# Attention in groups of two units, and no branch between two expert layers

## The chip, the cores and the metric

The kernel runs on one core of a Trainium2 chip. The metric is the device time of one execution in microseconds, as the median of several runs. The core has five engines that run beside each other, each through its own list of instructions in order: TensorE (matmuls; PE in the profile, with its weight loads as PEld), VectorE (DVE), ScalarE (ACT), GpSimd (POOL) and SyncE (SP), whose queue issues most of the DMAs. They wait for each other through semaphores.

## The reference

Three layers follow each other. The first is attention over 4 batches, 8 heads, 768 positions and 64 channels, with a window of 128 positions and 4 sink positions that every row sees:

```
keep = is_sink | in_window
scores = np.where(keep, scale * q @ k.T, -1e9)
a = softmax(scores)
x = (a @ v) as 3072 tokens of 512 channels
```

The second is a layer of 8 experts. Each token goes to the expert with the largest gate logit, and `out = gate * (relu(x @ w1[e]) @ w2[e])` with 1024 hidden channels. The third is such a layer again, but each expert takes exactly 384 tokens, in the order of all logits, largest first.

## The kernel before

**Attention** handles two heads (a pair) at a time: 16 pairs, and of each six blocks of 128 query rows. A block of a pair is a unit; there are 96. Two neighbouring units share an output tile and form a group; there are 48 groups. What is done for unit n is cut into steps, each a small function:

- `qk_mm` (line 291): scores of both heads on TensorE, 260 columns each (132 in the first unit of a pair), into one of two PSUM buffers `sp`;
- `mask_max` (lines 302 to 310): masks and row maximum on VectorE;
- `exp` (line 321): exponentials with row sums on ScalarE, which frees `sp`;
- `trans` (329): transposes of the exponentials into the PSUM tile `pt`; `sel` (335 to 340): copy of them to SBUF on ScalarE, and two selections on GpSimd that cut the window's lower and upper triangle into `lu`;
- `pv` (358): products of the values with `lu` into `po`;
- once a group: `sinkpack` (368), `sinktr` (375) and `sinkout` (380) for the sink columns, `outT` (386, copy of `po`), `rows` (396, 398, output rows and gate logits into the tile `px`), `xout` (412 to 418, division by the row sums on VectorE, store).

The order is written out by hand. A loop runs over units, and in each turn over a string of step names; each step has a lag in units, so that turn n does the scores of unit n, the exponentials of unit n-1, the transposes of unit n-2, the values products of unit n-6:

```
LM, LE, LT, LP, LK, LS, LO, LR = 0, 1, 2, 6, 3, 6, 8, 9
ORDER = "ex ld qk ini bg pv mm tr ro oT sp st xo so sq se"
```

So TensorE gets, for each unit, scores, values products, transposes, and then the group's output rows or the sink transpose. Two more steps are `ini`, which in the first turns prepares the sinks' values, and `bg`, which takes one piece of a background list (`BG`) in each of 108 turns. The list holds the setup of constants and, after each batch, the gate: logits, argmax, ranks, scatter of the token numbers; after the second batch also the table of the first experts' tiles, the gathers of their tokens, and one piece that loads their weights. What is left is taken in the first expert layer, two pieces at each tick while more than 12 are waiting.

**The first expert layer** (`moe1`) runs a static list of tiles. If an expert needs more tiles than the list has, further bodies run under a branch (line 1171) whose condition every engine loads from a table `tab`; with the inputs used here none of them runs. Then **the second expert layer** (`moe2`) selects the tokens by a search on VectorE with counts on TensorE (line 1375), loads the first expert's weights once its number is known, and runs the experts. At the end stands another branch, with a general version of the last layer that runs only if the search failed; it does not here.

Of the kernel before, what the change touches and what calls it, by code (L numbers as in the profile page):

```python
# [20 lines left out]
NB = S // 128  # L21
# [149 lines left out]
LM, LE, LT, LP, LK, LS, LO, LR = 0, 1, 2, 6, 3, 6, 8, 9  # L171
ORDER = "ex ld qk ini bg pv mm tr ro oT sp st xo so sq se"


def attention(ctx, tc, g, qT, kT, v4, vsT, vsR, wg, put_x, after_batch, bg, drain=True):
# [6 lines left out]
    NU = B * NP * NB  # L182
# [93 lines left out]
    st = {}  # L276

    def unit(n):
        p, i = divmod(n, NB)
        b, pr = divmod(p, NP)  # L280
        return b, pr, p, i

# [13 lines left out]
    def mask_max(n):  # L296
# [12 lines left out]
        s.mx = wk.tile([128, 2], F32, name="mx", bufs=3)  # L309
        nc.vector.tensor_reduce(s.mx, sp[:, :, 128:260], axis=AX.X, op=OP.max, negate=True)  # L310

    def exp(n):
        b, pr, p, i = unit(n)
        s = st[n]
        if i % 2 == 0:
            s.P = wk.tile([128, 2, 2, SEG], F32, name="P", bufs=4)
            s.sm = wk.tile([128, 2, 2], F32, name="sm", bufs=8)
        else:
            s.P, s.sm = st[n - 1].P, st[n - 1].sm
        for hd in range(2):  # L320
            nc.scalar.activation(s.P[:, i % 2, hd, :], s.sp[:, hd, 128:260], AF.Exp, bias=s.mx[:, hd:hd + 1],  # L321
                                 accum_out=s.sm[:, i % 2, hd:hd + 1])

    def trans(n):
        s = st[n]
        s.ptt = ps.tile([128, 512], F32, name="pt")
        s.pt = s.ptt[:, 0:256].rearrange("p (a c) -> p a c", a=2)
        for hd in range(2):
            nc.tensor.transpose(s.pt[:, hd, :], s.P[:, n % 2, hd, 4:132], g.ident)

    def sel(n):
        b, pr, p, i = unit(n)
        s = st[n]
        s.t = wk.tile([128, 2, 128], F32, name="t", bufs=3)
        nc.scalar.activation(s.t, s.pt, AF.Copy)
        s.lu = wk.tile([128, 2, 2, 128], F32, name="lu", bufs=8)
        nc.gpsimd.affine_select(s.lu[:, :, 0, :], s.t, pattern=[[0, 2], [1, 128]],
                                compare_op=OP.is_ge, fill=0.0, base=0, channel_multiplier=-1)
        if i:
            nc.gpsimd.affine_select(st[n - 1].lu[:, :, 1, :], s.t, pattern=[[0, 2], [-1, 128]],  # L340
                                    compare_op=OP.is_gt, fill=0.0, base=0, channel_multiplier=1)

    def pv(n):
        b, pr, p, i = unit(n)
        for j in ([i - 1] if i else []) + ([i] if i == NB - 1 else []):
            lu = st[n - i + j].lu
            if j == 0:
                st[p, 0] = ps.tile([128, 2, 128], F32, name="po", bufs=2)
            segs = [(0, 1)] if j == NB - 1 else ([(0, 2)] if j % 2 == 0 else [(0, 1), (1, 2)])
            for l0, l1 in segs:  # L350
                blk = j + l0
                gi = blk // 2
                if blk % 2 == 0 and l0 == 1:
                    st[p, gi] = ps.tile([128, 2, 128], F32, name="po", bufs=2)
                po = st[p, gi]
# [6 lines left out]
    def sinkpack(gn):  # L362
        s = st[2 * gn + 1]
        sk = psk[gn % 4]
        src = s.P[:, :, :, 0:4]
# [5 lines left out]
    def sinktr(gn, pt):  # L371
        s = st[2 * gn + 1]
        s.skp = (ps.tile([128, 512], F32, name="pt") if pt is None else pt)[0:96, 384:512]
        sk = psk[gn % 4]
        nc.tensor.transpose(s.skp, sk.bitcast(F32).rearrange("p a b c -> p (a b c)"), g.ident)

    def sinkout(gn):
        s = st[2 * gn + 1]
# [3 lines left out]
    def outT(gn):  # L382
        s = st[2 * gn + 1]
        p, gi = divmod(gn, 3)
        s.oT = wk.tile([128, 2, 128], F32, name="oT")
        nc.scalar.activation(s.oT, st[p, gi], AF.Copy)
# [3 lines left out]
    def rows(gn):  # L390
        s = st[2 * gn + 1]
        p, gi = divmod(gn, 3)
        b, pr = divmod(p, NP)
        s.px = ps.tile([128, 512], F32, name="px")
        px = s.px[:, 0:288].rearrange("p (a c) -> p a c", a=2)
        nc.tensor.matmul(px, s.skT, bd[:, p], start=True, stop=False, skip_group_check=True)
        for blk in range(2):
            nc.tensor.matmul(px[:, blk, :], s.oT[:, blk, :], rw[:, pr, :], start=False, stop=True,
                             skip_group_check=True)

    def xout(gn):
        s = st[2 * gn + 1]
        p, gi = divmod(gn, 3)
        b, pr = divmod(p, NP)
# [5 lines left out]
        px = s.px[:, 0:288].rearrange("p (a c) -> p a c", a=2)  # L410
# [5 lines left out]
                                px[:, :, 0:128].rearrange("p a (h d) -> p a h d", h=2),  # L416
                                bc(rv[:, :, :, None], [128, 2, 2, 64]), op=OP.mult)
        nc.vector.tensor_tensor(lp[:, i0:i0 + 2, h0:h0 + 2, :],
                                px[:, :, 128:144].rearrange("p a (h d) -> p a h d", h=2),
# [5 lines left out]

    def at(n, lag, last=NU):
        return n - lag if lag <= n < last + lag else None

    def sink(n, lag):
        m = n - lag  # L430
        return m // 2 if 0 <= m and m % 2 == 0 and m // 2 < NU // 2 else None

    def when(f, *a):
        return lambda n: None if f(n) is None else a[0](f(n))

    def loads(n):
        b, pr, p, i = unit(n)
        if i == 1:
            load_pair(p + 2)
            load_v(p + 1)  # L440

    def one_of(n, f):
        p, i = divmod(n, NB)
        f(p + 1, i)

    ops = dict(
        ld=when(lambda n: at(n, 0), loads),
        qk=when(lambda n: at(n, 0), qk_mm),
        mm=when(lambda n: at(n, LM), mask_max),
        ex=when(lambda n: at(n, LE), exp),  # L450
        tr=when(lambda n: at(n, LT), trans),
        se=when(lambda n: at(n, LT), sel),
        st=when(lambda n: sink(n, LS), lambda k: sinktr(k, st[2 * k + LS - LT].ptt if 2 * k + LS - LT < NU else None)),
        so=when(lambda n: sink(n, LS), sinkout),
        sp=when(lambda n: sink(n, LK), sinkpack),
        oT=when(lambda n: sink(n, LO), outT),
        ro=when(lambda n: sink(n, LR), rows),
        xo=when(lambda n: sink(n, LR), xout),
        pv=when(lambda n: at(n, LP), pv),
        sq=when(lambda n: at(n, 0), lambda n: one_of(n, scale_q)),  # L460
        bg=lambda n: bg.pop(1),
        ini=init)
    for n in range(NU + LR + 3):
        for op in ORDER.split():
            if op == "qk" and n < 6:
                warm(7 - n)
            ops[op](n)
# [10 lines left out]
class Gate:  # L478
    def __init__(self, tc, g, pool, mid, mbias, bg):
# [11 lines left out]
        self.tab = pool.tile([1, 3, NBIG + E], I32, name="tab")  # L491
# [601 lines left out]
def moe1(tc, g, G, src, rt, w1, w2, wg2, wg2T, x2d):  # L1093
    nc = tc.nc
    with ExitStack() as ctx:
# [4 lines left out]
        ids = src.ids  # L1100
        wgb = f.wk.tile([128, E, DM], F32, name="wgb", bufs=1)
        nc.sync.dma_start(wgb, bass.AP(tensor=wg2T.tensor, offset=wg2T.offset, ap=[[0, 128], [DM, E], [1, DM]]))
# [7 lines left out]
        def yout(j, a, y):  # L1110
            c = src.first(j)
            late = c - NMAIN if c is not None else -1
            yr = f.wk.tile([128, DM + E], F32, name=f"yr{(a + max(late, 0)) % 4}", bufs=1)
            lg = yr[:, DM:] if c is None else rt.LG[:, c + a]
            nc.scalar.activation(yr[:, 0:DM], y, AF.Copy, scale=src.gate(j, a))
            st = {}

            def dot(e):
                junk = f.wk.tile([128, DM], F32, name="junk")
                V.scalar_tensor_tensor(junk, yr[:, 0:DM], 1.0, wgb[:, e, :], op0=OP.mult, op1=OP.mult,  # L1120
                                       accum_out=lg[:, e:e + 1])
# [22 lines left out]
            def put():  # L1144
                nc.sync.dma_start(rt.xs[128 * (c + a):128 * (c + a) + 128, :], yr[:, 0:DM])

            def scatter():
                nc.gpsimd.indirect_dma_start(out=x2d, out_offset=bass.IndirectOffsetOnAxis(
                    ap=ids[j][:, a, 0:1], axis=0), in_=yr, in_offset=None, bounds_check=N - 1, oob_is_err=False)
            dots = [(lambda e=e: dot(e)) for e in range(E)]  # L1150
            if c is None:
                bg.add(*dots, scatter)
            elif j in static[:-3]:
                bg.add(put, *dots)
# [11 lines left out]
        def run(js, pre=None):  # L1166
            f.run(js, w1, w2, src, yout, hook=lambda: bg.pop(2 if len(bg.q) > 12 else 1), pre=pre, onx=onx, LEAD=2)

        run(static, (src.raw, dict(src.xg)))
# [742 lines left out]
```

## Time and profile before

| | |
|---|---|
| median of 3 runs | 937.57 us (936.87 to 937.63) |
| the profiled execution, its own time | 933.44 us |
| its span | 931.6 us |
| TensorE busy | 877.2 us, 94% |
| VectorE busy | 637.6 us, 68% |
| ScalarE busy | 419.8 us, 45% |
| GpSimd busy | 354.4 us, 38% |
| DMA, mean over the span | 133 GB/s |

The span is what the trace covers; the execution's own time lies 1.8 us above it. The shares are means over stages with different limits: attention ends at about 202 us, the first expert layer at about 539 us. In the trace a line such as L291 is a line of the kernel before, "x4" is the number of instructions in a row, `128*64` the part of the array that a matmul uses, and "<-PE sp L291" names what ended an engine's idle time. Matmuls are pipelined and their ends are modelled, so it is the starts that can be compared.

### The profile page before, as it was taken

The numbers are of one execution on the slowest core, as the hardware profiler recorded it, in microseconds if no ns is written. First come the engines' busy times: TensorE is split into PE (matmuls) and PEld (weight loads), VectorE is DVE, ScalarE is ACT, GpSimd is POOL, SyncE is SP. The second block draws the span as 40 slices with busy tenths as digits, with TensorE's granted clock in tenths as the row PEclk, the third lists the DMA queues.
The fourth block names the chain that finished last, engine by engine and source line by source line (L and its number), as shares of the span: only waits on it lengthen the run. The fifth ranks groups of instructions, "written<-read, shape, count | busy, mean of one in ns | idle before, by whom it ended". The sixth has DMA issues, their size and how long they took to land. (4 is left out here: it accounts for less than half of the span.)

```text
span 931.6 us, 15380 instructions
## 1 busy us (share of the span) xinstructions
PE 877.2 (94%) x5034; PEld 680.8 (73%) x5040; DVE 637.6 (68%) x1815; ACT 419.8 (45%) x1183; POOL 354.4 (38%) x600
## 2 busy tenths in 40 slices
PE   9999999988999999999998877999999998999993
PEld 4566666657888888888876635778888787789982
DVE  4878788757688878797954848878878777623220
ACT  4788887853333333343434504233424342344430
POOL 4676766753401010200000005536364563457441
PEclk9999999999999999999995979999999998999997
DMA  8244646394444444443443115326343442334201
GB/s 263 94 156 112 184 104 171 86 344 116 129 137 153 136 136 136 136 136 102 136 148 136 57 44 187 122 95 208 140 150 117 133 149 101 125 125 159 91 34 37
DMA packets 68951, 123.99 MB, mean 133 GB/s; under 512 B 9075, under 2 KB 21365, under 8 KB 68726
## 3 DMA queue, kind: packets, MB, share of 16 engines
q1 hardware_dynamic: 62166, 103.41, 34.8%
q0 software_dynamic: 6688, 19.43, 6.5%
q8 instruction: 44, 0.72, 0.3%
q14 instruction: 53, 0.43, 0.2%
HBM read 103.11 MB, written 19.71 MB: 132 GB/s over the span
## 5 line engine op out<-in xcount | busy, mean ns | idle before, releaser
L934 ACT ACTIVATE hh<-ph 128x384 fp32r<-128x384 f32 (+1 forms) x112 | 60.3, 538 | 270.9 <-PE ph L925 266.6
L925 PE MATMUL ph<-xh,w1h 128*128 128x384 f32 (+1 forms) x448 | 170.3, 380 | 0.0
L868 PE MATMUL y<-w2h,hh 128*128 128x512 f32 x400 | 163.8, 409 | 0.0
L925 PE MATMUL ph<-xh,w1l 128*128 128x384 f32 (+1 forms) x448 | 162.8, 364 | 0.0
L925 PE MATMUL ph<-xl,w1h 128*128 128x384 f32 (+1 forms) x448 | 161.9, 363 | 0.0
L868 PE MATMUL y<-w2h,hl 128*128 128x512 f32 x400 | 159.1, 398 | 0.0
L868 PE MATMUL y<-w2l,hh 128*128 128x512 f32 x400 | 159.0, 397 | 0.0
L935 DVE SCALAR_TENSOR_TENSOR hl<-ph,hh 128x384 fp32r<-128x384 f32 (+1 forms) x112 | 68.6, 612 | 109.6 <-ACT hh L934 106.7
L1080 POOL DMA_INDIRECT xg<-xd,ent x26 | 29.2, 1122 | 217.4 <-DMA ent<-idtab 118.9
L821 POOL TENSOR_TENSOR w2l<-w2r,w2h 128x512 fp32r<-128x512 f32 x64 | 87.5, 1372 | 53.3 <-ACT w2h L817 38.5
L1120 DVE SCALAR_TENSOR_TENSOR junk<-yr,wgb 128x512 f32<-128x512 f32 x160 | 103.6, 689 | 0.0
L925 PEld LDWEIGHTS ph<-xh,w1h 128*128 128x128 f32 x448 | 86.0, 192 | 10.7 <-issue 0.4
L925 PEld LDWEIGHTS ph<-xh,w1l 128*128 128x128 f32 x448 | 85.8, 192 | 9.6
L925 PEld LDWEIGHTS ph<-xl,w1h 128*128 128x128 f32 x448 | 85.2, 190 | 7.8
L868 PEld LDWEIGHTS y<-w2h,hl 128*128 128x128 f32 x400 | 76.3, 191 | 17.1 <-DVE hl L973 0.4
L868 PEld LDWEIGHTS y<-w2h,hh 128*128 128x128 f32 x400 | 76.7, 192 | 12.4 <-ACT hh L972 0.4
L868 PEld LDWEIGHTS y<-w2l,hh 128*128 128x128 f32 x400 | 76.6, 192 | 12.3 <-DVE w2l L821 0.3
L840 DVE TENSOR_TENSOR w1l<-w1r,w1h 128x512 fp32r<-128x512 f32 x96 | 73.6, 768 | 14.0 <-ACT w1h L835 13.0
L835 ACT ACTIVATE w1h<-w1r 128x512 fp32r<-128x512 f32 x128 | 79.7, 623 | 5.5 <-DMA w1r<-in_w_dram 2.8
L817 ACT ACTIVATE w2h<-w2r 128x512 fp32r<-128x512 f32 x128 | 79.4, 624 | 2.2 <-issue 2.2
L321 ACT ACTIVATE P<-sp,mx 128x132 f32<-128x132 f32 x192 | 69.0, 367 | 10.8 <-DVE mx L310 8.6
L840 POOL TENSOR_TENSOR w1l<-w1r,w1h 128x512 fp32r<-128x512 f32 x32 | 43.8, 1369 | 62.7 <-ACT w1h L835 62.7
(342 smaller groups left out, 1506.7 us busy)
## 6 DMA issues: line engine op xcount, KB each, us to landing
w1r<-in_w_dram SPq DMA_DIRECT2D x32, 1024.0 KB
w2r<-in_w_dram SPq DMA_DIRECT2D x32, 1024.0 KB
xs<-yr SPq DMA_DIRECT2D x26, 256.0 KB
kr<-in_kT_dram SPq DMA_DIRECT2D x16, 396.0 KB
qr<-in_qT_dram SPq DMA_DIRECT2D x16, 384.0 KB
vr<-in_v_dram SPq DMA_DIRECT2D x16, 384.0 KB
xd<-xb SPq DMA_DIRECT2D x16, 384.0 KB
wgb<-in_wg2T_dram SPq DMA_DIRECT2D x1, 2048.0 KB
```

The lines of the kernel that those rows point to most:

```text
L321: nc.scalar.activation(s.P[:, i % 2, hd, :], s.sp[:, hd, 128:260], AF.Exp, bias=s.mx[:, hd:hd + 1], accum_out=s.sm[:, i % 2, hd:hd + 1])
L817: nc.scalar.activation(ch[1][c][0], r[:, q, :], AF.Copy)
L821: eng.tensor_tensor(lo, r[:, q, :], h.bitcast(F32), op=OP.subtract)
L835: nc.scalar.activation(h, v, AF.Copy)
L840: eng.tensor_tensor(lo, v, h.bitcast(F32), op=OP.subtract)
L868: nc.tensor.matmul(o, l, r, start=(first and i == 0), stop=(end and i == 2))
L925: nc.tensor.matmul(ph, wp[:, c, :], xp_[:, c, 0:NTK], start=(d == 0 and i == 0), stop=(d == 3 and i == len(cut[d]) - 1))
L934: nc.scalar.activation(hh, ph, AF.Relu)
L935: nc.vector.scalar_tensor_tensor(hl, ph, 0.0, hh.bitcast(F32), op0=OP.max, op1=OP.subtract)
L1080: self.nc.gpsimd.indirect_dma_start(out=self.xg[j][:, a, :], out_offset=None, in_=self.G.xd[0:k, :], in_offset=bass.IndirectOffsetOnAxis(a ...
L1120: V.scalar_tensor_tensor(junk, yr[:, 0:DM], 1.0, wgb[:, e, :], op0=OP.mult, op1=OP.mult, accum_out=lg[:, e:e + 1])
```

## The change

The loop now runs over groups of two units. In each turn both units' scores are issued, then both masks and maxima, then the four transposes of the group before into one tile, with one copy of 512 elements between the two units' exponentials, the sink transpose and the output rows (which now share the tile `px`), and at the end both units' values products. The two selections of the lower triangle become one. The background list gives two pieces a turn, in 52 turns. The branch between the expert layers is gone: its bodies move into a function of their own, under the branch at the end.

```
-LM, LE, LT, LP, LK, LS, LO, LR = 0, 1, 2, 6, 3, 6, 8, 9
-ORDER = "ex ld qk ini bg pv mm tr ro oT sp st xo so sq se"
+LST, LPV, LRO = 3, 2, 4
...
+    def trans(k):
+        s = gr[k]
+        s.pt = ps.tile([128, 2, 2, 128], F32, name="pt")
+        for u in range(2):
+            for hd in range(2):
+                nc.tensor.transpose(s.pt[:, u, hd, :], s.P[:, u, hd, 4:132], g.ident)
+
+    def tcopy(k):
+        s = gr[k]
+        s.t = wk.tile([128, 2, 2, 128], F32, name="t")
         nc.scalar.activation(s.t, s.pt, AF.Copy)
...
+    def select(k):
+        b, pr, p, gi = group(k)
+        s = gr[k]
+        s.lu = wk.tile([128, 2, 2, 2, 128], F32, name="lu", bufs=4)
+        nc.gpsimd.affine_select(s.lu[:, :, :, 0, :].rearrange("p u h q -> p (u h) q"), s.t.rearrange("p u h q -> p (u h) q"),
+                                pattern=[[0, 4], [1, 128]], compare_op=OP.is_ge, fill=0.0, base=0, channel_multiplier=-1)
+        for u in range(2):
+            if u or gi:
+                o = s.lu[:, 0] if u else gr[k - 1].lu[:, 1]
+                nc.gpsimd.affine_select(o[:, :, 1, :], s.t[:, u], pattern=[[0, 2], [-1, 128]],
+                                        compare_op=OP.is_gt, fill=0.0, base=0, channel_multiplier=1)
...
+    for k in range(NG + LRO):
+        live = k < NG
+        px = None
+        if live:
+            if k % 3 == 0 and k:
+                load_pair(k // 3 + 2)
+                load_v(k // 3 + 1)
+            elif k == 0:
+                load_pair(2)
+                load_v(1)
+            begin(k)
+        at(outT, k - LRO)
+        at(sinkout, k - LRO)
+        if live:
+            for u in range(2):
+                if k < 3:
+                    warm(7 - 2 * k - u)
+                qk_mm(2 * k + u)
+                init(2 * k + u)
+            scale_q(k // 3 + 1, 2 * (k % 3))
+            for u in range(2):
+                mask_max(2 * k + u)
+        at(trans, k - 1)
+        if live:
+            exp(2 * k)
+        at(tcopy, k - 1)
+        if live:
+            exp(2 * k + 1)
+        at(sinkpack, k - 1)
+        bg.pop(2)
+        if 0 <= k - LST:
+            px = ps.tile([128, 512], F32, name="px")
+        at(sinktr, k - LST, px)
+        at(rows, k - LRO, px)
+        if 0 <= k - LPV < NG:
+            for u in range(2):
+                pv(2 * (k - LPV) + u)
+        at(select, k - 1)
+        at(xout, k - LRO)
...
-        with tc.If(nc.values_load(G.tab[0:1, 2, 2:3], min_val=0, max_val=1) > 0):
-            nbig = nc.values_load(G.tab[0:1, 2, 0:1], min_val=0, max_val=NBIG)
-            nsml = nc.values_load(G.tab[0:1, 2, 1:2], min_val=0, max_val=E)
...
     bad = moe2(tc, g, rt, w21, w22, out)
     with tc.If(bad > 0):
+        moe1_rest(tc, g, G, w1, w2, wg2T, x2d)
         moe2_general(tc, g, rt, x2d, w21, w22, out)
```

The steps `sinkpack`, `sinktr`, `outT`, `rows`, `xout` and `pv` do the same work as before, indexed by group. `moe1_rest` holds the bodies that stood under the removed branch, with weights and pools of its own.

## Rows read from the trace of the kernel before

**Rows 1.** Windows, 40 to 180 us: PE, PEld, DVE, ACT, POOL busy; clock; DMA.
```profile
40.00:180.00 140.00, 139.08 (x1072) 86.17 (x1070) 111.91 (x391) 112.33 (x486) 96.64 (x283) 1.00 0.52 137
```

**Rows 2.** Timeline, start of pair 2: start us, duration us, engine, line, operation.
```profile
34.82 0.50 PE L291 MATMUL sp<-kr,qs 64*128 64x132 f32 x4
```

**Rows 3.** Timeline of TensorE alone, 179 to 193 us.
```profile
179.87 0.87 PE L358 MATMUL po<-lu,vr 128*64 128x256 f32 x8
180.67 0.43 PE L329 MATMUL pt<-cst,P 128*128 128x128 f32 x2
...
181.66 0.49 PE L291 MATMUL sp<-kr,qs 64*128 64x132 f32 x4
182.09 0.44 PE L329 MATMUL pt<-cst,P 128*128 128x128 f32 x2
...
186.01 0.44 PE L329 MATMUL pt<-cst,P 128*128 128x128 f32 x2
...
186.49 0.71 PE L291 MATMUL sp<-kr,qs 64*128 64x260 f32 x4
187.13 0.65 PE L358 MATMUL po<-lu,vr 128*64 128x256 f32 x4
187.71 0.44 PE L329 MATMUL pt<-cst,P 128*128 128x128 f32 x2
...
188.12 0.65 PE L398 MATMUL px<-rw,oT 128*128 128x144 f32 x4
188.71 0.71 PE L291 MATMUL sp<-kr,qs 64*128 64x260 f32 x4
...
189.94 0.44 PE L329 MATMUL pt<-cst,P 128*128 128x128 f32 x2
...
192.26 0.66 PE L398 MATMUL px<-rw,oT 128*128 128x144 f32 x4
192.82 0.44 PE L329 MATMUL pt<-cst,P 128*128 128x128 f32 x2
```

**Rows 4.** Timeline between the two expert layers, VectorE and TensorE.
```profile
539.02 0.28 DVE L1369 TENSOR_TENSOR cmp<-ub,iou 128x128 bf16<-128x128 bf16 x1
...
542.80 0.92 PE L1375 MATMUL rt<-OH,cmp 128*128 128x16 bf16 x13 [2.94 <-DVEq L1171]
```

**Rows 5.** Timeline, one unit's mask to transposes, from two places.
```profile
105.00 0.43 DVE L310 TENSOR_REDUCE mx<-sp 128x2 f32<-128x264 f32 x1
...
105.47 0.37 ACT L321 ACTIVATE P<-sp,mx 128x132 f32<-128x132 f32 x1 [0.32 <-DVE mx L310]
...
106.08 0.20 ACT L321 ACTIVATION_READ_ACCUMULATOR P<-sp,mx 128x1 f32 x1
...
106.42 0.20 PEld L329 LDWEIGHTS pt<-cst,P 128*128 128x128 f32 x2 [0.17 <-ACT P L321]
...
189.53 0.43 DVE L308 COPY_PREDICATED sp<-msk,sp 128x256 f32<-128x256 int32 x1 [0.20 <-PE sp L291]
...
190.00 0.43 DVE L310 TENSOR_REDUCE mx<-sp 128x2 f32<-128x264 f32 x1
```

**Rows 6.** Groups by line and form: count, busy us, mean ns of one, idle before.
```profile
L337 POOL TENSOR_SCALAR_AFFINE_SELECT lu<-t 128x256 f32<-128x256 f32 x74 | 30.7, 415 | 41.0 <-ACT t L335 39.2 <-PE px L398 0.4
...
L335 ACT ACTIVATE t<-pt 128x256 f32<-128x256 f32 x75 | 28.2, 376 | 5.5 <-POOL psk L368 2.1 <-PE pt L329 1.0
...
L738 ACT ACTIVATE xh<-tr 128x512 fp32r<-128x512 f32 x21 | 12.6, 598 | 27.9 <-PE tr L737 27.9
```

**Rows 7.** Groups by line, two background pieces on VectorE, 40 to 180 us.
```profile
L553 DVE TENSOR_REDUCE lg<-lp 128x48 f32<-128x384 f32 x2 | 1.7, 863 | 0.1
L586 DVE TENSOR_TENSOR cb<-gpp,cb 128x8 f32<-128x8 f32 x10 | 1.7, 167 | 0.3
```

**Rows 8.** Windows, the same columns, 24 to 28 us.
```profile
24.00:28.00 4.00, 4.00 (x21) 1.81 (x19) 3.83 (x16) 2.85 (x13) 2.85 (x7) 0.53 0.02 7
```

**Rows 9.** Timeline of TensorE, start of the first expert layer.
```profile
212.43 0.20 PE L577 MATMUL rt<-oh,tri 128*128 128x48 bf16 x1 [3.79 <-DVE oh L568]
```

More of the change, by code (lines that the diff above doesn't have):

```diff
@@ L281, in unit, with group @@
         return b, pr, p, i
+    def group(k):
+        p, gi = divmod(k, NB // 2)
+        return p // NP, p % NP, p, gi
     def qk_mm(n):
@@ L308, in mask_max, with begin @@
             nc.vector.copy_predicated(own, bc(msk[:, 0:1, :], [128, 2, 128]), sp[:, :, 0:128])
-        s.mx = wk.tile([128, 2], F32, name="mx", bufs=3)
+        s.mx = wk.tile([128, 2], F32, name="mx", bufs=4)
         nc.vector.tensor_reduce(s.mx, sp[:, :, 128:260], axis=AX.X, op=OP.max, negate=True)
+    def begin(k):
+        s = gr[k] = K()
+        s.P = wk.tile([128, 2, 2, SEG], F32, name="P", bufs=3)
+        s.sm = wk.tile([128, 2, 2], F32, name="sm", bufs=8)
     def exp(n):
-        b, pr, p, i = unit(n)
@@ L314, in exp @@
[L314 to L319, printed above, removed]
-        for hd in range(2):
[L321 to L334, printed above, removed]
-        nc.scalar.activation(s.t, s.pt, AF.Copy)
[L336 to L341, printed above, removed]
+        s, z = st[n], gr[n // 2]
@@ L360, in pv, with sinkpack @@
                                      skip_group_check=True)
[L362 to L365, printed above, removed]
+    def sinkpack(k):
+        sk = psk[k % 4]
+        src = gr[k].P[:, :, :, 0:4]
         v = [sk[:, z, 0:4, :].rearrange("p (a b) c -> p a b c", b=2) for z in range(3)]
@@ L369, in sinkpack, with sinktr, sinkout, outT @@
         nc.gpsimd.tensor_tensor(v[1], src, v[0].bitcast(F32), op=OP.subtract)
[L371 to L378, printed above, removed]
+    def sinktr(k, px):
+        gr[k].skp = px[0:96, 384:512]
+        nc.tensor.transpose(gr[k].skp, psk[k % 4].bitcast(F32).rearrange("p a b c -> p (a b c)"), g.ident)
+    def sinkout(k):
+        s = gr[k]
         s.skT = wk.tile([96, 128], F32R, name="skT")
         nc.scalar.activation(s.skT, s.skp, AF.Copy)
-    def outT(gn):
-        s = st[2 * gn + 1]
-        p, gi = divmod(gn, 3)
+    def outT(k):
+        b, pr, p, gi = group(k)
+        s = gr[k]
         s.oT = wk.tile([128, 2, 128], F32, name="oT")
-        nc.scalar.activation(s.oT, st[p, gi], AF.Copy)
+        nc.scalar.activation(s.oT, pos[p, gi], AF.Copy)
     xl = {}
[L390 to L396, printed above, removed]
+    def rows(k, px):
+        b, pr, p, gi = group(k)
+        s = gr[k]
+        s.px = px[:, 0:288].rearrange("p (a c) -> p a c", a=2)
+        nc.tensor.matmul(s.px, s.skT, bd[:, p], start=True, stop=False, skip_group_check=True)
         for blk in range(2):
-            nc.tensor.matmul(px[:, blk, :], s.oT[:, blk, :], rw[:, pr, :], start=False, stop=True,
+            nc.tensor.matmul(s.px[:, blk, :], s.oT[:, blk, :], rw[:, pr, :], start=False, stop=True,
                              skip_group_check=True)
[L401 to L404, printed above, removed]
+    def xout(k):
+        b, pr, p, gi = group(k)
+        s = gr[k]
         if gi == 0:
@@ L424, in xout @@
                 after_batch(b, lp)
[L426 to L467, printed above, removed]
+    def at(f, k, *a):
+        if 0 <= k < NG:
+            f(k, *a)
+    for k in range(NG + LRO):
[37 more added lines that the diff above has]
+        at(xout, k - LRO)
@@ L1090, in xget, with gate_rows, dots, dot @@
         return self.xg[j]
-def moe1(tc, g, G, src, rt, w1, w2, wg2, wg2T, x2d):
+def gate_rows(nc, f, wg2T):
+    wgb = f.wk.tile([128, E, DM], F32, name="wgb", bufs=1)
+    nc.sync.dma_start(wgb, bass.AP(tensor=wg2T.tensor, offset=wg2T.offset, ap=[[0, 128], [DM, E], [1, DM]]))
+    return wgb
+def dots(nc, f, yr, wgb, lg):
+    def dot(e):
+        junk = f.wk.tile([128, DM], F32, name="junk")
+        nc.vector.scalar_tensor_tensor(junk, yr[:, 0:DM], 1.0, wgb[:, e, :], op0=OP.mult, op1=OP.mult,
+                                       accum_out=lg[:, e:e + 1])
+    return [(lambda e=e: dot(e)) for e in range(E)]
+def moe1_rest(tc, g, G, w1, w2, wg2T, x2d):
+    nc = tc.nc
+    with ExitStack() as ctx:
+        pool = ctx.enter_context(tc.tile_pool(name="m1rx", bufs=2))
+        src = Src1(nc, G, pool, w1, w2, None)
+        f = Ffn(ctx, tc, g, "m1r", tpe=TPE, rawpool=pool, vsplit=True)
+        wgb = gate_rows(nc, f, wg2T)
+        def yout(j, a, y):
+            yr = f.wk.tile([128, DM + E], F32, name="yr")
+            nc.scalar.activation(yr[:, 0:DM], y, AF.Copy, scale=src.gate(j, a))
+            for d in dots(nc, f, yr, wgb, yr[:, DM:]):
+                d()
+            nc.gpsimd.indirect_dma_start(out=x2d, out_offset=bass.IndirectOffsetOnAxis(
+                ap=src.ids[j][:, a, 0:1], axis=0), in_=yr, in_offset=None, bounds_check=N - 1, oob_is_err=False)
+        nbig = nc.values_load(G.tab[0:1, 2, 0:1], min_val=0, max_val=NBIG)
+        nsml = nc.values_load(G.tab[0:1, 2, 1:2], min_val=0, max_val=E)
+        for n, o, js in ((nbig, NE, range(SBIG, NE + NBIG)),
+                         (nsml, NE + NBIG, range(NE + NBIG + SSML, NE + NBIG + E))):
+            with ExitStack() as ifs:
+                for j in js:
+                    ifs.enter_context(tc.If(n > j - o))
+                    f.run([j], w1, w2, src, yout, LEAD=2)
+def moe1(tc, g, G, src, rt, w1, w2, wg2, wg2T):
     nc = tc.nc
@@ L1111, in yout @@
             c = src.first(j)
[L1112 to L1115, printed above, removed]
+            late = c - NMAIN
+            yr = f.wk.tile([128, DM], F32, name=f"yr{(a + max(late, 0)) % 4}", bufs=1)
+            lg = rt.LG[:, c + a]
+            nc.scalar.activation(yr, y, AF.Copy, scale=src.gate(j, a))
             st = {}
[L1118 to L1121, printed above, removed]
             def turn():
@@ L1144, in put @@
             def put():
[L1145 to L1154, printed above, removed]
+                nc.sync.dma_start(rt.xs[128 * (c + a):128 * (c + a) + 128, :], yr)
+            if j in static[:-3]:
+                bg.add(put, *dots(nc, f, yr, wgb, lg))
             else:
@@ L1164, in onx @@
                 bg.add(*rt.late_ids(static.index(j) - SBIG))
-        def run(js, pre=None):
-            f.run(js, w1, w2, src, yout, hook=lambda: bg.pop(2 if len(bg.q) > 12 else 1), pre=pre, onx=onx, LEAD=2)
-        run(static, (src.raw, dict(src.xg)))
+        f.run(static, w1, w2, src, yout, hook=lambda: bg.pop(2 if len(bg.q) > 12 else 1), pre=(src.raw, dict(src.xg)),
+              onx=onx, LEAD=2)
         bg.drain()
-        with tc.If(nc.values_load(G.tab[0:1, 2, 2:3], min_val=0, max_val=1) > 0):
-            nbig = nc.values_load(G.tab[0:1, 2, 0:1], min_val=0, max_val=NBIG)
-            nsml = nc.values_load(G.tab[0:1, 2, 1:2], min_val=0, max_val=E)
-            for n, o, js in ((nbig, NE, range(SBIG, NE + NBIG)),
-                             (nsml, NE + NBIG, range(NE + NBIG + SSML, NE + NBIG + E))):
-                with ExitStack() as ifs:
-                    for j in js:
-                        ifs.enter_context(tc.If(n > j - o))
-                        run([j])
-                        bg.drain()
 JC, NIT, FEW, IDLE = 64, 4, 2, 4
```

32 lines of the change are left out of this document (16 added, 16 removed).

## The prediction

> **What bounds the kernel now.** I read the windows first. From 40 to 180 us, which is attention in its steady state, TensorE is busy 139.08 of 140 us, the other engines between 97 and 112, and the granted clock is 1.00 [rows 1]. So TensorE's own sequence sets the pace there. The first unit of pair 2 starts at 34.82, that of pair 15 at 181.66 [rows 2, 3]: 13 pairs in 146.84 us, 11.30 us a pair, or 3.77 a group of two units.
>
> The timeline of TensorE shows what that sequence is made of; I read starts, since ends are modelled. A full group goes from 186.01 to 189.94, 3.93 us: transposes, sink transpose, scores, values products, transposes, rows, scores, values products [rows 3]. In it the array is not streaming all the time. A unit with 132 columns of scores keeps the next instruction away for 0.43 us (181.66 to 182.09), one with 260 for 0.64 (186.49 to 187.13): 128 columns cost 0.21, so 260 cost 0.43, and about 0.21 is left as a pause before the next kind of work. Values products: a unit's four matmuls of 256 columns take 0.58 (187.13 to 187.71). The eight at 179.87 are such four and, directly behind them, the four of 128 columns of a pair's last block; they take 0.80 (to 180.67). So 128 columns more cost 0.22, 256 cost 0.44, and 0.14 is pause, which the eight pay once. After the rows there is next to none: scores follow at 0.59 (188.12 to 188.71), and transposes, of the rows' own shape, follow at 0.56 (192.26 to 192.82).
>
> Last I read the timeline between the layers. The comparison that TensorE waits for ends at 539.30 on VectorE (539.02 and 0.28), and TensorE starts at 542.80, released by the queue of VectorE at line 1171, the branch [rows 4].
>
> **The change part by part.** *Order on TensorE.* A group now has six changes of kind, with pauses of 2 x 0.21 (after scores), 2 x 0.14 (after values) and 0.03 (after rows); I leave out the sink's. The new group has three: scores to transposes (0.21, as at 181.66, where the same change is seen), rows to values (taken as 0.03, the nearest row), values to scores. This last one is nowhere in the trace; between 0.03 and 0.21 I take 0.14, the pause that follows values now. So 0.73 becomes 0.38, 0.35 saved in a full group. In the first group of a pair one unit has no values products and 0.14 less to lose: 0.21 saved. A pair saves 2 x 0.35 + 0.21 = 0.91; with 14 pairs from pair 2 on, 12.7 us. Scores directly after scores are not in the trace either: at best no pause, as between the two values products, at worst 0.21, which costs 0.63 a pair. With both unknowns at their bad ends a pair saves 0.07, at their good ends 1.24: 1 to 17 us in all. I take 12.7, because inside one kind of work the only row that shows it has no pause.
>
> The Trainium skill (TensorEngine Tiling (Array Packing), section Tiling Modes) says that a change of tiling mode drains the array. The trace agrees after scores and values and hardly after rows (0.03). Were each of the three saved changes worth 0.21, as that sentence read alone would have it, a pair would save 1.9 and 14 pairs 26 us; the sum here goes by the rows.
>
> *The loop through the scores' two buffers.* Both units' scores are now issued together, so the second needs its buffer back from the group before. Counted from the start of the first scores: mask at +0.82 (188.71 to 189.53), maximum 0.47 later, exponentials 0.47 after that (105.00 to 105.47) [rows 5], so +1.76. The exponentials of a unit last to 106.28, 0.81 us, until +2.57. Then ScalarE does the merged copy of 512 elements: not in this stage, but 598 ns for the same shape elsewhere, against 376 for each of the two now [rows 6]. At +3.17 the second exponentials start (their maximum has been ready since +2.7), they end at +3.98, and TensorE sees it 0.14 later (106.28 to 106.42): +4.12. The new group is 3.93 - 0.35 = 3.58 us, and its second scores come 0.43 into the next one, at +4.01. The loop is thus 0.11 late; part of the delay carries over, so about 0.06 a group, 2.5 us in all. With exponentials that overlap, it is nothing. I take 1.
>
> *VectorE's queue.* In that loop VectorE is served in order: masks and maxima, then two background pieces, then the output rows of a group. Its own work is some 2.6 us a group (111.91 us over 37 groups is 3.0; 16 us of it in all I put down to background), with gaps 2.8; so 0.75 us a group is free. Now two pieces come at once instead of one per unit. A batch's chain has some 25 instructions, of 863 ns the dearest and mostly near 167 [rows 7], about 5 us, in four groups: roughly 1.5, 1.0, 0.8 and 2.1 us, 2.35 above what is free. Two batches fall into attention, 4.7, and the expert table's pieces there add some 2.5. Behind a late piece wait the next masks, behind them the exponentials, behind those TensorE's scores. 0 to 7 us; I take 4, since now such pieces are absorbed and then would be partly. The merged selects on GpSimd, the fewer copies on ScalarE (0.15 us a group) and the shared bank for sink and rows are costed at nothing: the copy ends at +3.17, three selects of 0.4 to 0.8 (0.41 for 256 elements now, [rows 6]) at +4.8, and the values products that read them start in the next group at about +6.0. Without that cover up to 1.6 us a group would go onto the path.
>
> *Start.* Initial pieces now stand in pairs ahead of both masks, so units 2 and 3 wait for the sinks' values together. VectorE is busy 3.83 of 4 us from 24 to 28 us [rows 8], and its sum of work stays: I take 1 us lost, 0 to 3.
>
> *Start of the first expert layer.* 108 background pops in attention become 104. Four more pieces stand ahead of the last batches' chains, so the matmul for which TensorE now waits 3.79 us at 212.43 [rows 9] is issued two ticks later, behind a further step of matmuls, while VectorE's chain goes on. 2 us back, 0 to 3.8. The weights' load (piece 41 of its batch) stays in the first iteration behind the last scores.
>
> *Branch.* Without it TensorE can start at about 539.4 in place of 542.80: 3.4 us. The chain after it (counts, comparisons, the first expert's number, weights) hangs on that start, so all of it moves. I take 3.3. The bodies that were skipped here now lie under the branch at the end, which is skipped as before: nothing.
>
> Sum: -12.7 + 1 + 4 + 1 - 2 - 3.3 = -12.0 us. The profiled execution took 933.44 us (span 931.6), so 921.4; the median of the runs is 937.57, 4.1 above it, so on the runs' scale 925.6. I say **925**.
>
> **Rivals.** *All pauses go and VectorE absorbs its pieces:* 17 from the pauses, nothing lost in the loop, 3.8 and 3.4: -24, 913. For it speaks that all engines but TensorE have 20% free [rows 1]; against it that no row shows scores after scores. By the rule of the Trainium skill cited above the pauses alone would give 26, and the time would be 904; the 0.03 after rows speaks against it, and I give it 0.03 of this case's chance.
>
> *The change does little of what it says:* scores pause after scores too, and the change back from values costs 0.21. Then 1 us from the pauses, the start loses 1, the branch gives 3.3: -3, 934. For it: the two row halves of the scores are another shape than all else, and each of its rows is followed by a pause; against it the values products at 179.87.
>
> *Slower: the clock.* TensorE runs at 1.00 in attention because nothing interrupts it; from 24 to 28 us the granted clock was 0.53 and 21 matmuls were done [rows 8], against 1072 in 140 us, 31 in 4 us. At that pace a group takes 3.77 x 31 / 21 = 5.5 us, 1.8 more than now. If the pairing of units leaves TensorE waiting in the start (it has no other scores to do while VectorE's initial pieces run) and the clock then stays at 1.2 GHz, the 12 us are gone after about 7 groups; at 14 groups the kernel is 12 us slower, 950. Against it: now the clock comes back within 8 us.
>
> **Numbers.** Forecast case 0.57, its own range 918 to 931; all pauses 0.2; little 0.11; slower 0.08; 0.04 for no change. The lower bound 913 keeps half of the second case, the upper 934 takes in the third. Of this kernel about 0.2% (1.9 us) can be told from no change: faster 0.57 + 0.2 + 0.11 = 0.88, same 0.04, slower 0.08.
>
> **What would show it.** In the profile after, groups start 3.4 to 3.7 us apart, against 3.77; scores follow scores at 0.43, not 0.64; TensorE's waits in attention are for exponentials, in groups with background pieces. The gap between the layers shrinks from 3.4 us to below 0.5, with the same chain behind it. I would be wrong if scores after scores start 0.64 apart, if TensorE waits more than 0.4 us in each group for exponentials or for the shared bank, if the granted clock is below 0.9 in any stretch from 40 to 180 us, or if the time between the layers only moves to the next wait.

## The result and the profile after

The changed kernel is slower: 940.50 us, median of 20 runs (936.24 to 945.47), against 935.12 for the kernel before in the runs beside it (928.79 to 942.86); the ratio is 1.0055, 95% interval 1.0035 to 1.0075. That is above the forecast of 925 and above the upper end of its range. The profiled execution took 943.73 us with a span of 942.0, 10.4 more than before.

The windows, in the columns of [rows 1]: attention's steady state, ten microseconds of it, and two shorter stretches that are used below.

```profile
40.00:180.00 140.00, 122.29 (x991) 86.30 (x991) 105.94 (x366) 94.23 (x411) 82.67 (x228) 0.95 0.50 130
80.00:90.00 10.00, 6.66 (x38) 4.91 (x37) 5.89 (x22) 4.03 (x17) 1.87 (x6) 0.66 0.24 79
83.50:88.70 5.20, 5.15 (x26) 3.64 (x26) 1.47 (x5) 1.28 (x6) 1.66 (x6) 0.53 0.28 79
134.00:139.50 5.50, 5.44 (x26) 3.64 (x26) 1.73 (x7) 1.29 (x6) 1.68 (x6) 0.50 0.26 74
```

TensorE is no longer busy throughout [rows 1]: 17.7 of 140 us are idle, and the granted clock, 1.00 before, is 0.66 in the second row. TensorE's timeline, around the start of a pair of heads without background pieces (the "quiet" pairs below), answers to [rows 2, 3]; the last two rows are the start of the last pair and the end of attention.

```profile
103.40 1.15 PE L294 MATMUL sp<-kr,qs 64*128 64x260 f32 x8
...
106.38 0.50 PE L294 MATMUL sp<-kr,qs 64*128 64x132 f32 x4
107.29 0.71 PE L294 MATMUL sp<-kr,qs 64*128 64x260 f32 x4 [0.41 <-ACT P L323]
107.93 0.66 PE L331 MATMUL pt<-cst,P 128*128 128x128 f32 x4
108.42 0.27 PE L380 MATMUL px<-cst,psk 128*96 128x128 f32 x1
...
109.25 1.09 PE L366 MATMUL po<-lu,vr 128*64 128x128 f32 x12
110.27 1.15 PE L294 MATMUL sp<-kr,qs 64*128 64x260 f32 x8
111.35 0.65 PE L331 MATMUL pt<-cst,P 128*128 128x128 f32 x4
...
191.65 0.50 PE L294 MATMUL sp<-kr,qs 64*128 64x132 f32 x4
...
209.79 0.65 PE L401 MATMUL px<-rw,oT 128*128 128x144 f32 x4
```

Between the kinds of work the order does what was forecast. Two units' scores take 1.08 (110.27 to 111.35), which is two times 0.43 and one pause of 0.21: scores after scores have none. Twelve values products (as many columns as eight of 256) take 1.02, which is 0.88 and the pause of 0.14. One thing was not forecast: in the first group of a pair the second unit's scores start 0.91 after the first's (106.38 to 107.29), whose 132 columns take 0.22, so 0.69 goes to a wait for exponentials. Between neighbouring quiet pairs lie 10.50 us (34.88, 45.35, 55.87, 66.37), against 11.18 to 11.21 before. But the pairs are not all quiet. Pair 6 starts at 77.53 and pair 7 at 95.68: 18.15 us; pair 10 takes 18.57. Pairs 5, 7, 9, 11 and 13 take 10.7 to 13.3. So pair 15 starts 10 us later than before, and the last row matmul ends at 210.44 instead of 201.55.

Pairs 6 and 10 hold the pieces v2 to v4 of a batch's gate (v2 starts with the exponential, v3b has the two matmuls that give ranks, v4 the slots), which the background queue now gives out two at a time, behind both units' masks and exponentials. The timeline of pair 6, three engines:

```profile
78.45 0.26 ACT L563 ACTIVATE ex<-dl 128x48 f32<-128x48 f32 x1
...
78.74 0.24 DVE L564 TENSOR_SCALAR dl<-dl 128x48 f32<-128x48 f32 x1 [1.48 <-ACT ex L563]
...
80.82 0.18 DVE L419 TENSOR_TENSOR lp<-px,rv 128x32 f32<-128x32 f32 x1
...
81.11 0.27 ACT L385 ACTIVATE skT<-px 96x128 fp32r<-96x128 f32 x1 [2.13 <-DVE lp L419]
...
81.44 0.18 PE L579 MATMUL px<-oh,tri 128*128 128x48 bf16 x1 [1.51 <-ACT skT L385]
...
83.28 0.22 DVE L582 COPY gpp<-px 128x96 f32<-128x96 f32 x1
...
83.55 0.45 PE L380 MATMUL px<-cst,psk 128*96 128x128 f32 x1 [1.90 <-DVE gpp L582]
...
85.13 1.98 PE L366 MATMUL po<-lu,vr 128*64 128x128 f32 x12
...
88.39 0.43 DVE L311 COPY_PREDICATED sp<-msk,sp 128x256 f32<-128x256 int32 x1 [2.63 <-PE sp L294]
```

Read it as a relay. VectorE stands 1.48 us in a piece, because the gate's exponential comes behind the turn's four exponentials in ScalarE's queue. The row reads (xb, lp) come behind the piece, and ScalarE's sink copy, which reads the same bank, comes behind them (2.13). The gate's rank matmuls need that bank (1.51); their copy to gpp is behind three mask steps, two maxima and three steps of the gate, and TensorE waits again (1.90). Behind these 3.4 us of standing the granted clock is near 0.5 (0.53 from 83.5 to 88.7, the lower level of 1.2 GHz): twelve values products take 1.98 in place of 1.09, and from the sink transpose to the next transposes it is 5.2 us where the quiet pair's steps add up to 2.9 (sink transpose at 108.42 to scores at 110.27, and 1.08). The same stretch in pair 10 takes 5.5, at a clock of 0.50: some 4.9 us for both.

The start of the first expert layer and the gap between the layers, answering to [rows 9] and [rows 4]:

```profile
224.59 0.18 PE L579 MATMUL rt<-oh,tri 128*128 128x48 bf16 x1 [2.70 <-DVE oh L570]
...
238.54 0.20 PE L579 MATMUL rt<-oh,tri 128*128 128x48 bf16 x1 [1.13 <-DVE oh L570]
...
550.39 0.28 DVE L1389 TENSOR_TENSOR cmp<-ub,iou 128x128 bf16<-128x128 bf16 x1
...
551.28 0.89 PE L1395 MATMUL rt<-OH,cmp 128*128 128x16 bf16 x13
```

From the comparison's end to the second layer's first matmul it is now 0.61 us, against 3.50. The wait of [rows 9] is 2.70 us, from 3.79; but the same matmul of the next batch's gate, which waited 0.06 before, now waits 1.13, so the two together wait 3.8 us as before.

The 10.4 us of span, by stage: attention to its last row matmul +8.9; to the first expert matmul +0.3; the first layer's matmuls +2.2; the gap between the layers -2.9; the second layer +1.2; the tail +0.7.

### The profile page after: what moved, and what is told of

Read it like the earlier page. It is cut to its first block, busy times and chain, and to the rows that moved or that the text cites. A ratio compares the mean times of both kernels' runs of the same rounds, so it can differ in the third digit from the quotient of the medians.

```text
span 942.0 us, 15311 instructions
## 1 busy us (share of the span) xinstructions
PE 865.3 (92%) x5035; PEld 688.7 (73%) x5040; DVE 639.8 (68%) x1815; ACT 407.8 (43%) x1135; POOL 346.8 (37%) x552
## 4 chain that ended last, share of the span: by engine, by line
PE 70%; DVE 15%; issue 5%; ACT 4%; POOL 3%; DMA 1%; SPq 0%; POOLq 0%; DVEq 0%; ACTq 0%
PE ph L927 25%; PE y L870 25%; PE sp L294 3%; PE po L366 3%; PE tr L739 2%; DVE sc L150 2%; PE rt L1395 2%; ACT P L323 2%; DVE cmp L150 2%; PE pt L331 2%; PE px L401 1%; PE rc L1258 1%; DVE w1l L842 1%; DVE ohb L150 1%; DMA vsx<-in_vsR_dram 1%
## 5 line engine op out<-in xcount | busy, mean ns | idle before, releaser
L294 PE MATMUL sp<-kr,qs 64*128 64x260 f32 (+1 forms) x384 | 58.9, 408 | 9.8 <-ACT P L323 9.7
```

Of the source, the lines that this page charges most:

```text
L294: nc.tensor.matmul(sp[:, hd, c0:260], qs[o:o + 64, 128 * i:128 * i + 128], kr[o:o + 64, k0:k0 + 260 - c0], start=True, stop=True)
```

## The experiments

**Measure.** Attention's length is taken from each trace: from the first scores of pair 2 to the end of the last row matmul, on TensorE. It is 166.7 us before (34.82 to 201.55) and 175.6 after (34.88 to 210.44), and kernels with the same attention agree within 0.6. The whole time scatters by some 3 us from run to run, so ratios to before have intervals of 0.2 to 0.5% on either side.

My first theory was the **shared bank**: ScalarE waits 15.5 us (8 times) for VectorE's last row read, since sink and rows now share a bank. The rivals were pieces taken **in pairs**, and a loss behind attention.

| run | what it is | attention, us | ratio to before (95%) |
|---|---|---|---|
| e1_branch_alone | before, branch moved | 166.5 | 0.9995 (0.9972 to 1.0018) |
| e16_branch_again | the same | 166.5 | 0.9992 (0.9965 to 1.0019) |
| e2_groups_alone | after, old branch | 175.0 | 1.0142 (1.0104 to 1.0179) |
| e3_sink_first | after, sink copy ahead of the row reads | 181.6 | 1.0126 (1.0084 to 1.0169) |
| e4_before_pairs | before, pieces in pairs | 171.8 | 1.0074 (1.0048 to 1.0100) |
| e5_spread | after, a piece ahead of each mask | 161.9 | 0.9906 (0.9877 to 0.9935) |
| e15_spread_again | the same | 162.2 | 0.9899 (0.9862 to 0.9937) |
| e14_spread_old_branch | the same, old branch | 162.2 | 0.9946 (0.9920 to 0.9972) |
| e6_sink_bank | after, sink in the values' bank | 180.2 | 1.0111 (1.0057 to 1.0164) |
| e7_spread_sink | e5 and e6 | 166.6 | 0.9945 (0.9908 to 0.9982) |
| e8_pairs_early | after, pairs ahead of both masks | 166.6 | 0.9954 (0.9916 to 0.9992) |
| e9_rank_bank | after, rank matmuls in another bank | 174.6 | 1.0056 (1.0021 to 1.0092) |
| e10_exp_early | after, gate's exponential a piece earlier | 172.0 | 1.0020 (0.9989 to 1.0050) |
| e11_both_late | e9 and e10 | 171.5 | 1.0002 (0.9964 to 1.0039) |
| e12_spread_exp | e5 and e10 | 161.2 | 0.9910 (0.9871 to 0.9950) |
| e13_pairs_behind_rows | after, pairs behind the row reads | 166.4 | 0.9994 (0.9962 to 1.0026) |

**Each half alone** (e1, e16, e2). The old attention with the new fallback at the end; the new attention with the old branch.

> The kernel before with only the fallback of the first expert layer moved to the end; attention in its old order. If the loss sits in attention (theory), the branch's removal alone makes the kernel 3 to 5 us faster than before (0.995 to 0.997): VectorE's comparison to the second layer's first matmul took 3.5 us before and 0.6 us after. If instead what follows attention got slower by the change (rival), this kernel stays within 1 us of before.

> The new attention with the old branch between the layers. Theory: the whole loss is attention's, so 8 to 11 us slower than before (1.009 to 1.012), with its last row of scores where the changed kernel has it. Rival (the loss lies in the layers behind): within 2 us of before.

The loss is attention's: e2 has all of it, e1 none. The branch is less plain. In all 14 traces without it, from the first layer's last matmul to the second's first takes 4.97 or 4.98 us, in the four with it 7.75 to 7.87. Yet e1 is not measurably faster.

**The shared bank** (e3, e6). e3 moves ScalarE's copy of the sink ahead of VectorE's reads:

```diff
-        at(sinkout, k - LRO)
...
         at(select, k - 1)
+        at(sinkout, k - LST)
         at(xout, k - LRO)
```

> The changed kernel, with ScalarE's copy of the sink transpose issued one turn earlier, ahead of VectorE's reads of the output rows in the same bank. Theory of the shared bank: ScalarE's waits for the last of those reads (15.5 us in 8 waits) go, and with them the TensorE stalls behind them; 9 to 14 us faster than the changed kernel, so 0.991 to 0.997 of before, and the pairs of heads that hold pieces of the gate come near the quiet ones' 10.5 us. Rival (two pieces of the gate at a time are too much for VectorE in a turn, whatever the bank): at most 3 us faster than the changed kernel, the pairs with pieces stay at 18 us.

It missed: 6.0 us more of attention, pair 6 still at 18.1, and quiet pairs at 10.9 to 11.3. Turning the order round only lets the other engine wait. e6 takes the sharing away: the sink transpose goes into free columns of the values' bank.

```diff
-        gr[k].skp = px[0:96, 384:512]
+        gr[k].skp = pos[p, gi][0:96, 2, :]
...
                 pv(2 * (k - LPV) + u)
+        at(sinktr, k - LST)
```

> The changed kernel with the sink transpose in free columns of the values' bank, behind the values' products, where only ScalarE reads; pieces stay where the change put them. Theory of the shared bank: ScalarE's waits for VectorE's last row read (15.5 us in 8) go and attention falls by 5 to 10 us, from 175.5 to 165 to 170. Rival (the place of the pieces): those waits go too, but at most 3 us come off, since VectorE's masks stand behind the same pieces.

ScalarE's waits for the row reads are gone, and attention is 4.6 us longer: quiet pairs take 10.8 (the transpose is now one more change of kind, behind the values), the last pair's start to the end 20.6 instead of 18.8, pairs 6 and 10 still 18.0 and 18.5. The view of waits for e6 (total, times, longest) shows TensorE itself at the late row reads and the late rank copy:

```profile
PE px L400 <- DVE gpp L583: 4.6, 2, 2.3
...
PE px L400 <- DVE lp L420: 3.2, 3, 1.3
DVE dl L565 <- ACT ex L564: 3.0, 2, 1.5
...
PE px L580 <- DVE lp L420: 2.3, 2, 1.1
```

So the theory of the shared bank falls: the bank was where the lateness was passed on, not where it came from. The Trainium skill (PSUM — Partial Sum Buffer, section PSUM bank collisions raise a hardware error) asks that engines be kept apart by bank and quadrant, not by address; the trace agrees, since sink and rows are read from different columns and one read waited 2.13 us for the other.

**Pairs or place** (e4, e5, e8, e7).

```diff
e4:  -        bg=lambda n: bg.pop(1),
     +        bg=lambda n: bg.pop(2) if n % 2 else None,
e5:             for u in range(2):
     +              bg.pop(1)
                    mask_max(2 * k + u)
     ...
     -      bg.pop(2)
e8:  +  bg.pop(2)
     +  if live:
            for u in range(2):
                mask_max(2 * k + u)
     ...
     -      bg.pop(2)
```

> The kernel before with its background pieces taken two at a time in every second unit instead of one in each. Theory of the shared bank: the old kernel's sink copy reads a bank that VectorE does not, so two pieces at a time cost it at most 1.5 us (within 0.2% of before). Rival (pieces in pairs are the loss): 5 us or more slower than before, the pairs of heads with pieces longer.

> The changed kernel with its background pieces taken one ahead of each unit's mask, as the kernel before does, instead of two behind both units' exponentials. Theory of the place: the gate's exponential no longer stands behind four others on ScalarE, and the copy that frees the shared bank no longer behind four mask steps on VectorE; attention from the third pair to its last row matmul falls from 175.5 us to 160 to 166, so 0.990 to 0.996 of before. Rival (the bank shared by sink and rows is the loss): at most 4 us off the changed kernel, 171 us or more.

> The changed kernel with its background pieces still two at a time, but ahead of both masks. Theory of the place: attention falls to 163 to 170 us, short of the spread pieces by about the 5 us that pairs cost the old order. Rival (two pieces at a time are the loss): no shorter than the changed kernel's 175.5 us by more than 2.

> Both edits together: pieces one ahead of each mask, and the sink transpose in the values' bank. If the two causes add, attention takes 157 to 160 us (12 quiet pairs at 10.5 and a drain), 0.988 to 0.993 of before. If one of them is all of the loss, the time is that of the better of the two alone.

e4 went against me too: pairs cost the old order 5.0 us. In the new one they cost 4.7 (166.6 to 161.9), and the place, late or early, costs 9.0 (175.6 to 166.6). e7 adds e6's loss to e5's gain. Pair 6 of e5, the same steps as above:

```profile
79.70 0.18 DVE L419 TENSOR_TENSOR lp<-px,rv 128x32 f32<-128x32 f32 x1
...
80.09 0.28 ACT L385 ACTIVATE skT<-px 96x128 fp32r<-96x128 f32 x1
...
80.65 0.20 PE L581 MATMUL px<-oh,tri 128*128 128x48 bf16 x1
...
81.34 0.25 DVE L584 COPY gpp<-px 128x96 f32<-128x96 f32 x1
...
81.65 0.32 PE L380 MATMUL px<-cst,psk 128*96 128x128 f32 x1 [0.29 <-DVE gpp L584]
...
80.00:90.00 10.00, 9.11 (x78) 6.41 (x79) 9.17 (x35) 6.50 (x28) 5.54 (x16) 1.00 0.23 74
```

Between the rank matmuls and their copy VectorE now has a mask step and a maximum, TensorE waits 0.29 instead of 1.90, and the window (last row) keeps the clock at 1.00 with VectorE busy 9.17 of 10 us instead of 5.89.

**What of the place costs** (e9, e10, e11, e12, e13). e9 gives the rank matmuls the transposes' bank, e10 issues the gate's exponential at the end of v1b, e13 pops behind xout:

```diff
e9:  -    g.pst = lambda: ps.tile([128, 512], F32, name="px")
     +    g.pst = lambda: ps.tile([128, 512], F32, name="pt")
e10: (v1b)  +    nc.scalar.activation(ex, dl, AF.Exp)
     (v2)   -    nc.scalar.activation(ex, dl, AF.Exp)
e13: -        bg.pop(2)
     ...
              at(xout, k - LRO)
     +        bg.pop(2)
```

> The changed kernel with the gate's two rank matmuls in the transposes' bank instead of the bank of sink and rows; pieces stay late and in pairs. Theory of the place, first half (TensorE's next sink transpose waits 1.9 us for the rank copy behind four masks, and the clock falls to half behind that pause): the heads' pairs that took 18.2 and 18.6 us fall to 13 to 15, attention from 175.5 to 166 to 170 us, and the granted clock stays at full. Rival (VectorE's bursts alone set the loss): under 2 us off attention, the clock falls all the same.

> The changed kernel with the gate's exponential issued at the end of the piece before, one turn earlier, so that VectorE does not wait for it (1.48 us before the next step). Theory of the place, second half: the pair of heads that holds it gets 1 to 2 us shorter, attention 172 to 174 us; if the pause of TensorE that drops the clock begins with this wait, 166 to 170 us and a full clock. Rival (the wait is hidden): 175 us or more.

> Both: rank matmuls in the transposes' bank and the gate's exponential one piece earlier, pieces still late and in pairs. If the place costs what it does through these two waits, attention comes to 164 to 168 us, level with the pairs taken early (166.6 us). If it stays above 171 us, the place costs by something else (masks late behind a burst of pieces).

> Pieces one ahead of each mask, and the gate's exponential one piece earlier. The two pairs of heads of 12.2 us come to 11 to 12 us, attention to 160 to 162 us from 162.0; 0.988 to 0.991 of before. If the spread had already hidden that wait, no difference to the spread pieces alone (0.9906).

> The changed kernel with its background pieces still two at a time, but behind VectorE's reads of the output rows, at the turn's end. If the loss of the late place is that pieces run ahead of those reads, so that the bank of sink and rows comes free late while VectorE later idles for scores, attention comes to 165 to 169 us, level with the pairs ahead of the masks (166.6). If it is the queues of ScalarE and TensorE that count (the gate's exponential and rank matmuls behind the turn's own), it stays at 171 to 175 us.

e9 missed (1.0 us, and the granted clock from 80 to 90 us was 0.69), e10 gave 3.5, e11 4.1 of the 9.0, and e13 as much as e8 (166.4 and 166.6; in the time e13 reads 0.9994 and e8 0.9954, their intervals overlapping). e9 does not take TensorE's wait away: in the other bank the first rank matmul waits 3.35 us for ScalarE's copy of the transposes, nearly as long as the two waits of 1.51 and 1.90 together, and in e11 2.15, as the rows show. So neither run prices that wait. e13 says more of it: there too that matmul waits 2.06 us, with a clock of 0.66 from 85 to 90 us, and still pair 6 takes 11.6: one such wait with one such fall is not the loss. With pieces already spread, e12 has 0.8 us less of attention than e5, which the times don't show. The timelines of e9 (first row) and e11: the rank matmuls, and behind them a group whose scores are done while VectorE is still in the pieces and the row reads.

```profile
84.80 0.20 PE L579 MATMUL pt<-oh,tri 128*128 128x48 bf16 x1 [3.35 <-ACT t L336]
...
82.40 0.20 PE L579 MATMUL pt<-oh,tri 128*128 128x48 bf16 x1 [2.15 <-ACT t L336]
...
90.81 1.15 PE L294 MATMUL sp<-kr,qs 64*128 64x260 f32 x8
...
91.67 0.17 DVE L596 SCALAR_TENSOR_TENSOR slot<-gsm 128x6 int32<-128x6 f32 x1
...
91.89 0.66 PE L331 MATMUL pt<-cst,P 128*128 128x128 f32 x4
...
92.55 0.18 DVE L419 TENSOR_TENSOR lp<-px,rv 128x32 f32<-128x32 f32 x1
92.65 0.42 DVE L311 COPY_PREDICATED sp<-msk,sp 128x256 f32<-128x256 int32 x1
92.83 0.28 ACT L385 ACTIVATE skT<-px 96x128 fp32r<-96x128 f32 x1 [2.22 <-DVE lp L419]
```

A late pair of pieces holds up two things at once, the row reads (and with them TensorE's bank) and the next masks; pieces on the other side of the row reads hold up the masks alone. That the place ahead of the row reads is the cost is shown by e8 and e13. How the 9.0 us divide between TensorE's wait for the rank matmuls, late rows, late masks and the clock, which in e11 too was 0.66 from 80 to 90 us, is not shown.

**The branch in the time** (e14, e15, e16).

> Spread pieces with the old branch between the layers. Attention 162 us as with the branch moved; 2.9 us from the first layer's last matmul to the second's first come back, so 2 to 4 us slower than the same attention without the branch, 0.993 to 0.996 of before. Rival (the branch is worth nothing in the time): equal to it within 1 us.

> The spread pieces without the branch once more, beside the same attention with it: 0.990 to 0.992 of before, 2 to 4 us under it.

> The kernel before with only the branch moved, once more: 0.996 to 0.998 of before if the 2.9 us seen between the layers reach the end; 0.999 to 1.001 if not, as the first reading of it (0.9995, 0.9972 to 1.0018) leaves open.

With the spread order the branch is worth 0.4 to 0.5% (0.9946 against 0.9906 and 0.9899, intervals overlapping), with the old order 0.1% (twice, 2.5 us of uncertainty each). 2.9 us is 0.3% and lies within all of these, but the timings alone don't show that it reaches the end; nor do they explain why e2 reads 0.9% above the changed kernel with the same attention. The traces show a part that does not: from TensorE's last matmul to the end of the span it takes 15.1 us in the four traces with the branch and 15.6 to 16.1 in the 14 without, so 0.5 to 1.0 us are lost again at the end, where the skipped bodies now lie.

## Why the prediction was wrong

**The step that failed** is "VectorE's queue", taken as +4, at most +7. With no more stall from pieces than the old order had, the new attention would take 166.7 less 9.0 (13 pairs at 0.69) less 1.1 (from the last pair's start to the last row matmul 18.8 instead of 19.9): 156.6. It took 175.6, so the term measured **+19.0**, by e8 and e5: 9.0 for the place, 4.7 for the pairs, and, by subtraction, 5.3 that remain when pieces are spread as before (e5, 161.9). My 4 was the price of the last part only. I counted the pieces' durations against VectorE's free time and asked what stood behind a late piece on VectorE. I did not ask what the piece itself waits for in its new place (ScalarE's queue), nor what TensorE owes to it (the rank matmuls in a bank that TensorE needs at once), nor where in VectorE's turn the free time lies: it is the wait for scores, and pieces behind the masks come after it.

**"The shared bank ... costed at nothing"** was wrong as a wait: 15.5 us of ScalarE's, and up to 6.9 of TensorE's weight loads behind it. As a cause it was close to nothing: without the sharing (e6) pairs 6 and 10 keep 18.0 and 18.5 us of 18.15 and 18.57, though the quiet ones grow by 0.3, so it is worth some 0.4 us in each of the two; and with the pieces in the right place the sharing stays and the waits fall to 1.4 us.

**Order on TensorE, and the loop.** The mechanism of the pauses was right and the values taken (0 for scores after scores, 0.14 after values) were measured, so 0.91 us a pair stands. Two sizes beside it were wrong, in opposite directions. The sink transposes, left out of the sum, save too: transposes, sink transpose and rows take 1.32 us a group (107.93 to 109.25), and took 0.48 and 1.00 (186.01 to 186.49 and 187.71 to 188.71 in [rows 3]), some 0.48 less a pair. The loop, taken as 1 us in all, costs 0.69 in each pair (0.41 of it idle by the profile at 107.29). It was worked out for a full group of 3.58 us, but the last group of a pair, with four values products, takes 2.98 (103.40 to 106.38), and the scores behind it have 132 columns; there the exponentials are late. What is left, 0.91 and 0.48 less 0.69, is the 0.69 to 0.70 that a quiet pair saved; that it is near the 0.84 of the two terms (12.7 less 1, over 14 pairs) is luck. The Trainium skill's sentence on draining (TensorEngine Tiling (Array Packing), section Tiling Modes), read alone and priced at 0.21 a change, would have made it 1.9 us a pair; the trace shows 0.91 for them (0.21 after scores and 0.14 after values in a full group), and 0.48 more with the sink's.

**Start**: pair 2 begins at 34.88 against 34.82, so nothing, not 1; over all traces it begins between 34.0 and 39.2, with the old order alone between 34.0 and 38.0. **First expert layer**: nothing back, not 2: the wait of 3.79 us became two of 2.70 and 1.13. **Branch**: 2.9 in the gap, 3.3 forecast, and 0.5 to 1.0 lost at the end, which was put at nothing; open in the time.

**The slower rival** had the right kind of event in the wrong place. The clock did fall, not in the start and not for half the kernel, but in two groups, at a price of 4.9 us, behind waits that the pieces made. My own sign of being wrong (a clock under 0.9 between 40 and 180 us) was met.

With the pieces ahead of the masks the same change gives 0.990 to 0.991 of before (e5, e12, e15), some 9 us faster; the forecast's 12 were not reached by any of the kernels.

## What to carry to other kernels

When an order is regrouped, the small work that rides along is regrouped too: before costing it by its duration, write down for each piece what it waits for in its new place, who waits for it, and whether it stands before or after the time in which its engine idles anyway. Moving a few small steps across one group of reads was worth 9.0 us here, nearly all that the reordering gained (10.1). And when one engine waits long for another over a shared buffer, test the lateness of the other's work first: taking the sharing away left the two slow pairs at 18.0 and 18.5 us. A loop of waits is costed for the shortest group that runs through it: here the full group hid 0.69 us a pair, and the total came out near only by luck.

## What was not expected of the hardware

The first expert layer, the same matmuls in all 18 traces, took from 325.8 us to 338.7 from its first matmul to its last. Most of it runs alike; toward its end the granted clock differs from execution to execution. Here are the same two stretches of the layer in e15 and then in e13, first some 240 us of its middle, then the rest of it.

```profile
238.40:478.50 240.10, 240.10 (x1097) 198.76 (x1096) 190.88 (x484) 92.96 (x171) 21.48 (x18) 1.00 0.44 138
478.50:524.50 46.00, 38.68 (x190) 29.29 (x188) 31.93 (x96) 25.47 (x49) 0.00 (x0) 0.89 0.37 120
```

```profile
250.20:490.70 240.50, 240.50 (x1097) 198.73 (x1096) 190.74 (x484) 92.96 (x170) 19.82 (x18) 1.00 0.43 137
490.70:544.60 53.90, 45.98 (x190) 35.04 (x189) 32.19 (x96) 25.59 (x49) 0.00 (x0) 0.72 0.31 103
```

The same 190 matmuls took 46.0 us and 53.9, at a clock of 0.89 and 0.72; in e5, the same kernel as e15, 50.8 at 0.76. Another 2.6 us between e15 and e13 lie ahead of the first stretch. This last stretch has many short waits, and whether the clock falls in one of them differs even between executions of one kernel; that this is the scatter of some 3 us in the times is argued, not shown. It is as large as the branch's gain, which is why stages had to be compared in the traces.
